# Two cached attention layers, decode step: VectorE's code made shorter, probability sums in 128-column matmuls, the last values loaded in five pieces

## The chip, the cores and the metric

The kernel runs on one core of one Trainium2 chip. A core has five engines with their own instruction streams: TensorE (PE; its weight loads are listed as PEld), VectorE (DVE), ScalarE (ACT), GpSimd (POOL) and SyncE (SP). Sixteen DMA engines carry its transfers. The metric is the device time of one execution in microseconds (us). Before the change the median of four runs is 441.03 us (440.8 to 441.29).

## The reference

Two layers of grouped-query attention for one new token each (batch 4, 32 query heads, 8 key/value heads, 128 wide) over a cache of 8192 positions. Layer A reads the whole cache, layer B only its last W = 2048 positions. Both outputs are put side by side.

```python
q = (x @ wq) split into heads                       # x: [4, 1, 512], wq: [512, 4096]
k, v = cache, repeated for the 4 query heads of each key/value head
scores = einsum("bhqd,bhkd->bhqk", q, k) * 128 ** -0.5
p = softmax(scores)
o = einsum("bhqk,bhkd->bhqd", p, v) @ wo            # wo: [4096, 512]
```

All inputs are bfloat16. Keys and values of layer A are 134 MB, of layer B (the window) 34 MB, the four weight matrices 17 MB: 184.56 MB are read in all.

## The kernel before, in words

The work is cut into 20 units. Units 0 to 3 are layer B, one batch entry each with all eight key/value heads; units 4 to 19 are layer A, one pair of key/value heads of one batch entry each. A unit reads 4 MB of keys (`K_sb`) and 4 MB of values (`V_sb`), each in one of two slots. Its 128 tiles hold 64 positions of two heads.

Per unit, TensorE transposes the keys through PSUM (`pe_T`, line 278), eight tiles a job; VectorE and ScalarE take turns in copying them to `KT_sb` (lines 286 and 287). TensorE forms the scores against the unit's queries (`pe_S`, line 309) in the banks `SA` and `SB`. VectorE takes the maxima (line 411), GpSimd combines them over the partitions (line 432), VectorE subtracts (lines 439 and 449), and ScalarE takes the exponential into `PT` (line 460). One unit later TensorE adds up the probabilities against a matrix of ones (`pe_SM`, line 337; 16 matmuls of `NW = 64` columns, four accumulation groups), VectorE reduces that to a sum per head (`dve_sum`, line 467, `LB` from 256 columns) and inverts it (line 474), TensorE multiplies probabilities and values (`pe_PV`, line 325), and VectorE normalizes (`add_norm`, lines 482 to 497). A turn is two units. Each turn also turns eight heads' outputs (`pe_job_OT`, `pe_job_OL`; copies at lines 354 and 374) and multiplies them with a piece of `wo` (`pe_job_OPJ`, line 387, added up in `oacc` at line 395). In the turns 0 to 2 there is no piece yet, and these jobs work on zeros.

The order of every engine's work is written out by hand in `plan` (one list per engine). `emit_loop` (line 817) emits it: TensorE's ten turns are a hardware loop; VectorE and ScalarE run turns 0 to 2 unrolled and turns 3 to 9 as a loop. GpSimd's and SyncE's code is unrolled throughout. At the end of each turn a loop subtracts the turn's count from every semaphore that it waits on, with one instruction per semaphore (line 883). A wait that is implied by an earlier wait of the same engine on the same semaphore is not emitted.

Ahead of the first unit stands the set-up. GpSimd clears buffers and makes the identity matrices (lines 513 to 531). VectorE writes the masks and the permutation matrix (lines 533 to 554), and copies the Q projection out of PSUM: `xT` (line 203), `QT` (line 226, four jobs per layer) and `RQ` (line 248, four casts per layer). The Q weights lie in the slots of `V_sb` meanwhile, so that the first values can be loaded only when their projection is done (line 721).

SyncE issues all large loads in one queue, in the order K of the unit, then V of the unit before (lines 745 to 763). A K load waits until the slot's keys have been transposed (`T`) or its older unit has been normalized (`otr`), a V load waits for `otr` of two units before. The values of the last unit come in four transfers (`VCH = [4, 2, 1, 1]`, line 682, in eighths of 4 MB), each with a semaphore of its own, then eight transfers of 128 KB with the last piece of `wo` (`Wl_sb`). After the loops TensorE runs PV of the last unit in eight chunks, each waiting for its transfer; ahead of the fifth chunk it adds the probabilities (`pe_SM(L)`) and loads `oacc` into the accumulators (`pe_seed`). Then come the last normalization (line 488), 16 matmuls with `Wl_sb` (line 699), two copies (lines 703 and 704) and two output transfers.

Of the kernel before, what the change touches and what calls it, by code (L numbers as in the profile page):

```python
# [9 lines left out]
ACTF = mybir.ActivationFunctionType  # L10
# [4 lines left out]
def bass_concat_heads__gqa_block_cached__sliding_block_cached__decode_kernel(  # L15
# [33 lines left out]
    scale = float(DH) ** -0.5  # L49
    NKT = 4  # L50
    NW = 64
    NBK = 4
    NFILL = 3
    NTH = NT // 2
# [16 lines left out]
    with ExitStack() as es:  # L71
# [8 lines left out]
        def sm(name):  # L80
# [39 lines left out]
        KTB = [ps("KT%d" % i, 512) for i in range(NBK)]  # L120
        OTB = ps("OT", 512)

        names = ["k0", "k1", "kh", "v0", "v1", "vl0", "vl1", "vl2", "vl3", "wl0", "wl1", "wl2", "wl3", "wl4", "wl5", "wl6", "wl7", "x0", "x1", "w0", "w1", "wo",
                 "out0", "out1", "out2", "Tq", "Td", "Ta", "S", "PV", "Ed", "Ea", "Eq", "max", "sub", "sum", "rcp", "exp", "otr", "os", "otp",
                 "ocp", "Ef", "fin0", "fin1", "ar1", "SM", "maxc", "pset", "setup", "pm0", "pm1", "oc", "ocB", "mk0", "mk", "mka", "perm", "rq"]
        sems = {n: sm("s_" + n) for n in names}

        K_sbf = K_sb.bitcast(F32)
# [6 lines left out]
        def sem_of(key):  # L135
            t = key[0]
            if t in ("K", "Kh"):
                return sems["k%d" % (key[1] % 2)]
            if t in ("V", "Vh"):
                return sems["v%d" % (key[1] % 2)]  # L140
            if t == "T":
                j = jobs[key[1]]
                return sems["Tq" if j["turn"] is None else "Td" if j["eng"] == "dve" else "Ta"]
            if t == "pm":
                return sems["pm%d" % key[2]]
            if t == "KH":
                return sems["kh"]
            if t in ("VL", "WL", "x", "out", "fin"):
                return sems["%s%d" % (t.lower(), key[1])]
            if t == "WQ":  # L150
                return sems["w%d" % key[1]]
            if t == "E":
                if jobs[key[1]]["turn"] is None:
                    return sems["Eq"]
                return sems["Ed"] if jobs[key[1]]["eng"] == "dve" else sems["Ea"]
            return sems[t]

        DMA_KEYS = ("K", "Kh", "KH", "V", "Vh", "VL", "WL", "x", "out", "WQ", "wo", "mk")

# [28 lines left out]
            return KTB[jobs[idx]["bank"]]  # L188

        def pe_job_xT(P):  # L190
            idx = xt_idx[P] = new_job("xT", "dve")
            bk = kbank(idx).bitcast(BF16)

            def fn(pe):
                ins = None
                for c in range(DC):
                    ins = pe.transpose(out=bk[:, c * 8:c * 8 + Bn], in_=x_sb[0:Bn, P, :].rearrange("b (p c) -> b c p", c=DC)[:, c, :],  # L197
                                       identity=ident[0:Bn, 0:Bn])
                return ins
            op("pe", fn, waits=[("x", P), ("setup",), bankfree(idx)], inc=("T", idx))  # L200

            def efn(dve):
                return dve.tensor_copy(out=xT[:, P, :, :],
                                       in_=bk[:, 0:DC * 8].rearrange("p (c b) -> p c b", c=DC)[:, :, 0:Bn])
            add(dict(eng="dve", fn=efn, waits=[("T", idx)], inc=("E", idx)))

        def wq_view(P):
            return V_sb[:, 1 - P, :, :].rearrange("p t d -> p (t d)").rearrange("p (c n) -> p c n", c=DC)

        def pe_job_QP(P, i):  # L210
            idx = qp_idx[(P, i)] = new_job("QP", "dve")
            bk = kbank(idx)
            wv = wq_view(P)

            def fn(pe):
                ins = None
                for hl in range(HQJ):
                    hq = i * HQJ + hl
                    for c in range(DC):
                        ins = pe.matmul(out=bk[:, hl * Bn:(hl + 1) * Bn], lhsT=wv[:, c, hq * DH:(hq + 1) * DH],  # L220
                                        rhs=xT[:, P, c, :], start=(c == 0), stop=(c == DC - 1))
                return ins
            op("pe", fn, waits=[("WQ", P), ("E", xt_idx[P]), bankfree(idx)], inc=("T", idx))

            def efn(dve):
                return dve.tensor_copy(out=QT[:, P, :, i * HQJ:(i + 1) * HQJ],
                                       in_=bk[:, 0:HQJ * Bn].rearrange("p (h b) -> p b h", b=Bn))
            add(dict(eng="dve", fn=efn, waits=[("T", idx)], inc=("E", idx)))

        def pe_job_perm(P):  # L230
            idx = perm_idx[P] = new_job("perm", "dve")
            bk = kbank(idx)

            def fn(pe):
                ins = None
                for e in range(2):
                    ins = pe.matmul(out=bk[:, e * Bn * HQ:(e + 1) * Bn * HQ],
                                    lhsT=permE[:, e, :, :].rearrange("p t i -> p (t i)"),
                                    rhs=QT[:, P, :, :].rearrange("p b h -> p (b h)"), start=True, stop=True)
                return ins  # L240
            op("pe", fn, waits=[("E", qp_idx[(P, NQP - 1)]), ("perm",), bankfree(idx)], inc=("T", idx))

            def efn(dve):
                ins = None
                for e in range(2):
                    for tl in range(2):
                        src = bk[64 * tl:64 * tl + 64, e * Bn * HQ:(e + 1) * Bn * HQ]
                        ins = dve.tensor_copy(
                            out=RQ[P][64 * tl:64 * tl + 64, :, :, e, C * tl:C * tl + C],
                            in_=src.rearrange("p (b g c) -> p b g c", b=Bn, g=NSEG))  # L250
                return ins
            add(dict(eng="dve", fn=efn, waits=[("T", idx)], inc=("E", idx)))

        def pe_filler(n):
            bank = (jobs[-1]["bank"] + 1) % NBK
# [74 lines left out]
        def pe_SM(u):  # L330
            def fn(pe):
                ins = None
                for s in range(NSEG):
                    n = TS * C // NW
                    for i in range(n):
                        c0 = s * TS * C + i * NW
                        ins = pe.matmul(out=SA[u % 2][:, s * NW:(s + 1) * NW], lhsT=onesb[:, :], rhs=PT[:, u % 2, c0:c0 + NW],  # L337
                                        start=(i == 0), stop=(i == n - 1))
                return ins
            op("pe", fn, waits=[("exp", u) if u >= 0 else None], inc=("SM", u))  # L340
# [18 lines left out]
        def pe_job_OL(tn):  # L359
# [9 lines left out]
            op("pe", fn, waits=[("E", ot_idx[tn]), bankfree(idx)], inc=("T", idx))  # L369

            def efn(dve):
                ins = None
                for h in range(REP):
                    ins = dve.tensor_copy(
                        out=OL[32 * h:32 * h + 32, :, :, :],
                        in_=bk[32 * h:32 * h + 32, 0:REP * NR].rearrange("p (r g h b) -> p g h r b", r=REP, g=2, h=REP)[:, :, h, :, :])
                return ins
# [85 lines left out]
        def dve_sum(u):  # L463
            S, n = nseg(u), ncol(u)

            def fn(dve):
                return dve.tensor_reduce(out=LB[:, 0:n].rearrange("p (s h) -> p s h", h=C),
                                         in_=SA[u % 2][:, 0:NSEG * NW].rearrange("p (s j h) -> p s h j", s=S, h=C),
                                         axis=AX.X, op=AluOpType.add)
            return dict(eng="dve", fn=fn, waits=[("SM", u)], inc=("sum", u))  # L470

# [32 lines left out]
        def pool_otp(tn):  # L504
# [5 lines left out]
                w.append(("otr", 2 * tn - 2))  # L510
            return dict(eng="pool", fn=lambda pool: pool.tensor_copy(out=OTp[:, :, :], in_=OT_sb[:, P, q, :, :]), waits=w, inc=("otp", tn))

        def pool_setup0(pool):
            pool.memset(dummy[:, :], 0.0)
            pool.memset(onesf[:, :], 1.0)
# [4 lines left out]
            pool.memset(oacc[:, :], 0.0)  # L520
            pool.memset(PT[:, :, :], 0.0)
            return pool.memset(Wo_sb[:, :, :, :], 0.0)
        op("pool", pool_setup0, inc=("pset",))

        def pool_setup1(pool):
            ins = pool.affine_select(out=ident[:, :], in_=onesb[:, :], pattern=[[1, 128]],
# [3 lines left out]
            return ins  # L530
        op("pool", pool_setup1, waits=[("pset",)], inc=("setup",))

        def dve_setup0(dve):
            mkv = MK[:, :].rearrange("p (g s h) -> p g s h", g=NSEG, s=2)
            dve.memset(mkv[0:64, :, 0, :], 0.0)
            dve.memset(mkv[0:64, :, 1, :], -BIG)
            dve.memset(mkv[64:128, :, 0, :], -BIG)
            return dve.memset(mkv[64:128, :, 1, :], 0.0)
        op("dve", dve_setup0, inc=("mk0",))

        def dve_setup1(dve):
            dve.memset(MASK[0][0:64, 0:REP], 0.0)
            dve.memset(MASK[0][0:64, REP:C], -BIG)
            dve.memset(MASK[0][64:128, 0:REP], -BIG)
            return dve.memset(MASK[0][64:128, REP:C], 0.0)
        op("dve", dve_setup1, inc=("mka",))

        def dve_setup2(dve):
            ins = None
            for e in range(2):  # L550
                for tl in range(2):
                    ins = dve.tensor_copy(out=permE[:, e, tl, :], in_=ident[:, :].rearrange("p (i e) -> p e i", e=2)[:, e, :])
            return ins
        op("dve", dve_setup2, waits=[("setup",)], inc=("perm",))
        for sh in range(2):
            m0 = MASK[1][:, :]
            pstm = m0.ap[0][0]
# [121 lines left out]
            return ins  # L679
        add(dve_sum(L))  # L680
        add(dve_rcp(L))
        VCH = [4, 2, 1, 1]
        vch_of = [i for i, n in enumerate(VCH) for _ in range(n)]
        for c in range(NC):
            w = [("VL", vch_of[c])]
# [246 lines left out]
```

## Time and profile before

| what | value |
|---|---|
| median of four runs | 441.03 us (440.8 to 441.29) |
| profiled execution, its own time | 441.43 us |
| its span, first to last instruction | 439.6 us |
| granted TensorE clock, mean | 0.957 |
| read from HBM | 184.56 MB, 420 GB/s over the span |
| VectorE, line 286, 160 copies | 110.5 us, 690 ns each |
| VectorE, line 467, 20 reductions | 8.4 us, 418 ns each |
| VectorE, line 411 on `SB`, 20 reductions | 13.8 us, 692 ns each |
| VectorE, line 374, 40 casts | 7.4 us, 184 ns each |
| VectorE, line 226, 8 casts | 1.5 us, 192 ns each |
| VectorE, line 248, 8 casts | 2.3 us, 288 ns each |
| TensorE, line 337, 336 matmuls | 13.2 us, 192 ns each (they overlap) |

The span is the stretch between the first and the last instruction of the profiled execution; 1.83 us of its time lie around it. Busy times are summed per group of instructions. Matmuls are pipelined, so their durations overlap. Instructions are fetched by DMA too: the list of DMA queues shows them as kind "instruction". The trace also holds a record of every single DMA packet (start, duration, size and queue), and each transfer ends with a four-byte completion write from each DMA engine that took part in it.

### The profile page before, as it was taken

What the parts mean: (1) busy time and instruction counts of PE and PEld (TensorE: products, weight loads), DVE (VectorE), ACT (ScalarE), POOL (GpSimd) and SP (SyncE); (2) the same over time, 40 slices, a digit from 0 to 9 for tenths busy, and PEclk for the clock granted to TensorE, in tenths of its full rate; (3) what the DMA queues carried; (4) which work ended last, traced back from release to release, by engine and by line L of the source; (5) the groups of instructions that cost most, each with busy time, mean ns of one, the idle gap of its engine ahead of it and who ended that gap; (6) DMA issues with size and microseconds to landing.
All of it is one profiled execution on the core that took longest, in us unless ns stands there. A gap on an engine that the chain in (4) does not pass through costs nothing.

```text
span 439.6 us, 15852 instructions
## 1 busy us (share of the span) xinstructions
PE 365.5 (83%) x7312; PEld 337.2 (77%) x7312; DVE 210.2 (48%) x462; ACT 189.7 (43%) x203; POOL 27.8 (6%) x84
## 2 busy tenths in 40 slices
PE   0068998998997958895989698969878895989986
PEld 0068897997996948795979688968878794979975
DVE  0034455654664634463555346625653563555641
ACT  1004473473563625271636263534534361636530
POOL 6100000000000000000000000000100000000000
PEclk9999999999999988998899799969998998899999
DMA  8999999999999999999999999999999999999995
GB/s 341 421 416 419 418 418 420 422 444 409 448 429 432 416 441 429 432 424 435 429 435 423 430 438 425 433 432 429 414 445 432 435 423 436 429 429 413 446 407 210
DMA packets 13253, 184.76 MB, mean 420 GB/s; under 512 B 1412, under 2 KB 2488, under 8 KB 4536
## 3 DMA queue, kind: packets, MB, share of 16 engines
q1 hardware_dynamic: 13152, 184.56, 99.0%
q8 instruction: 8, 0.13, 0.1%
q14 instruction: 5, 0.04, 0.0%
q0 software_dynamic: 64, 0.02, 0.0%
q10 hardware_dynamic: 24, 0.01, 0.0%
HBM read 184.56 MB, written 0.01 MB: 420 GB/s over the span
## 4 chain that ended last, share of the span: by engine, by line
DMA 46%; PE 45%; PEld 4%; issue 2%; DVE 1%; SPq 1%; PEldq 0%
DMA K_sb<-in_A_k_cache_dram 35%; PE KT L278 23%; PE OT L325 9%; DMA K_sb<-in_B_k_cache_dram 7%; DMA V_sb<-in_A_v_cache_dram 4%; PE SA L309 4%; PE SB L309 4%; PE KT L387 3%; PEld KT L278 2%; SPq L566 1%; PE SA L337 1%; PE KT L325 1%; DVE oacc L395 1%; PEld OT L325 1%; PEld SA L309 1%
## 5 line engine op out<-in xcount | busy, mean ns | idle before, releaser
L278 PE MATMUL KT<-identf,K_sb 128*128 128x128 f32 x1280 | 207.5, 296 | 45.1 <-DMA K_sb<-in_A_k_cache_dram 34.0
L287 ACT ACTIVATE KT_sb<-KT 128x1024 bf16<-128x1024 bf16 x160 | 163.2, 1024 | 137.8 <-PE KT L278 137.8
L278 PEld LDWEIGHTS KT<-identf,K_sb 128*128 128x128 f32 x1280 | 146.9, 149 | 50.6 <-DMA K_sb<-in_A_k_cache_dram 35.3
L286 DVE COPY KT_sb<-KT 128x512 int32<-128x512 int32 x160 | 110.5, 690 | 120.8 <-PE KT L278 119.3
L325 PE MATMUL OT<-PT,V_sb 128*128 128x64 bf16 x2560 | 78.1, 193 | 2.1 <-DMA V_sb<-in_A_v_cache_dram 1.2
L325 PEld LDWEIGHTS OT<-PT,V_sb 128*128 128x128 bf16 x2560 | 75.9, 98 | 2.4 <-DMA V_sb<-in_A_v_cache_dram 1.3
L460 ACT ACTIVATE PT<-Dt 128x512 bf16<-128x512 f32 x40 | 24.6, 631 | 80.5 <-DVE Dt L449 80.5
L309 PEld LDWEIGHTS SA<-RQc,KT_sb 128*128 128x128 bf16 x1280 | 57.0, 98 | 2.4
L309 PEld LDWEIGHTS SB<-RQc,KT_sb 128*128 128x128 bf16 x1280 | 50.6, 97 | 7.9 <-issue 4.4
L309 PE MATMUL SA<-RQc,KT_sb 128*128 128x16 bf16 x1280 | 56.4, 170 | 0.0
L309 PE MATMUL SB<-RQc,KT_sb 128*128 128x16 bf16 x1280 | 52.8, 170 | 0.0
L411 DVE TENSOR_REDUCE M<-SB 128x8 f32<-128x512 f32 (+1 forms) x20 | 13.8, 692 | 50.3 <-PE SB L309 50.3
L432 POOL PARTITION_ALL_REDUCE MB<-M1m x20 | 7.7, 387 | 334.8 <-DVE M1m L425 334.8
L387 PE MATMUL KT<-Wo_sb,OL 128*4 128x512 bf16 x80 | 18.9, 379 | 0.0
L197 PE MATMUL KT<-ident,x_sb 4*128 4x4 bf16 x8 | 0.6, 170 | 20.8 <-POOL identf L528 20.8
L197 PEld LDWEIGHTS KT<-ident,x_sb 4*128 4x128 bf16 x8 | 0.4, 113 | 21.0 <-issue 21.0
L449 DVE TENSOR_TENSOR Dt<-SA,MBm 128x512 f32<-128x512 f32 x20 | 13.8, 691 | 0.7
L449 DVE TENSOR_TENSOR Dt<-SB,MBm 128x512 f32<-128x512 f32 x20 | 13.6, 681 | 0.0
L411 DVE TENSOR_REDUCE M<-SA 128x8 f32<-128x512 f32 (+1 forms) x20 | 13.6, 681 | 0.0
L337 PE MATMUL SA<-PT,onesb 128*128 128x64 bf16 x336 | 13.2, 192 | 0.0
L387 PEld LDWEIGHTS KT<-Wo_sb,OL 128*4 128x4 bf16 x80 | 6.0, 84 | 8.1
L337 PEld LDWEIGHTS SA<-PT,onesb 128*128 128x128 bf16 x336 | 11.1, 97 | 0.0
(72 smaller groups left out, 125.7 us busy)
## 6 DMA issues: line engine op xcount, KB each, us to landing
K_sb<-in_A_k_cache_dram SPq DMA_DIRECT2D x15, 4096.0 KB, 22.7
V_sb<-in_A_v_cache_dram SPq DMA_DIRECT2D x15, 4096.0 KB, 30.8
K_sb<-in_B_k_cache_dram SPq DMA_DIRECT2D x16, 1024.0 KB, 22.8
V_sb<-in_B_v_cache_dram SPq DMA_DIRECT2D x16, 1024.0 KB, 19.4
V_sb<-in_B_wq_dram SPq DMA_DIRECT2D x1, 4096.0 KB, 12.6
V_sb<-in_A_wq_dram SPq DMA_DIRECT2D x1, 4096.0 KB, 22.5
Wo_sb<-in_B_wo_dram SPq DMA_DIRECT2D x4, 1024.0 KB, 11.8
K_sb<-in_A_k_cache_dram SPq DMA_DIRECT2D x2, 2048.0 KB, 18.5
```

Of the source, the lines that this page charges most:

```text
L278: ins = pe.transpose(out=bkf[:, pi * 128:(pi + 1) * 128], in_=K_sbf[:, slot, t0:t0 + 2, :].rearrange("p t d -> p (t d)"), identity=identf[ ...
L286: return e.tensor_copy(out=KT_sb.bitcast(I32)[:, tj % NKT, :], in_=bkf.bitcast(I32)[:, :])
L287: return e.activation(out=KT_sb[:, tj % NKT, :], in_=bk[:, :], func=ACTF.Copy)
L309: ins = pe.matmul(out=stb[:, t % NTH * C:(t % NTH + 2) * C], lhsT=ktv[:, pi, :, e], rhs=RQc[:, u % 2, t // TS, e, :], start=(e == 0), stop ...
L325: ins = pe.matmul(out=otb[:, s * NW:s * NW + w], lhsT=V_sb[:, slot, t, :], rhs=PT[:, slot, t * C:t * C + w], start=(j == 0), stop=(j == n ...
L337: ins = pe.matmul(out=SA[u % 2][:, s * NW:(s + 1) * NW], lhsT=onesb[:, :], rhs=PT[:, u % 2, c0:c0 + NW], start=(i == 0), stop=(i == n - 1))
L387: ins = pe.matmul(out=bk[0:Bn, 0:D], lhsT=OL[:, i // REP, i % REP, :], rhs=Wo_sb[:, i // REP, i % REP, :], start=(i == 0), stop=(i == C - 1))
L395: return dve.tensor_tensor(out=oacc[:, :], in0=bk[0:Bn, 0:D], in1=oacc[:, :], op=AluOpType.add)
L411: return dve.tensor_reduce(out=M1[:, h * n:(h + 1) * n].rearrange("p (s h) -> p s h", h=C), in_=bank[:, :].rearrange("p (s j h) -> p s h j ...
L432: return pool.partition_all_reduce(MB[:, 0:n], M1m[:, 0:n], channels=128, reduce_op=ReduceOp.max)
L449: return dve.tensor_tensor(out=Dt[:, h * NTH * C:(h + 1) * NTH * C].rearrange("p (s j h) -> p s j h", s=Sh, h=C), in0=bank[:, :].rearrange ...
L460: return act.activation(out=PT[:, u % 2, a:b], in_=Dt[:, a:b], func=ACTF.Exp, scale=scale)
```

## The change

The 12 set-up instructions of VectorE (masks and permutation matrix) go to GpSimd; the mask writes stand ahead of its other set-up, the permutation copies behind the identity matrices. The Q projection's copies out of PSUM go to ScalarE, and the four casts to `RQ` become two. In the turns without a piece of `wo`, the four copies to `OL` become one of the same number of elements. The semaphores `max`, `maxc`, `sum`, `rcp` and `os`, with which VectorE waits for itself, become one, `vs`. The probability sums go in 8 matmuls of `NM = 128` columns in place of 16 of 64, and the reduction behind them reads 512 columns in place of 256. The last values come in five transfers, `[2, 2, 2, 1, 1]`.

```diff
+    NM = 128
...
-                 "out0", ..., "Eq", "max", "sub", "sum", "rcp", "exp", "otr", "os", "otp",
+                 "out0", ..., "Eq", "vs", "sub", "exp", "otr", "otp",
...
-            return sems[t]
+            return sems["vs" if t in ("max", "maxc", "sum", "rcp", "os") else t]
...
-            def efn(dve):
-                return dve.tensor_copy(out=QT[:, P, :, i * HQJ:(i + 1) * HQJ],
-                                       in_=bk[:, 0:HQJ * Bn].rearrange("p (h b) -> p b h", b=Bn))
-            add(dict(eng="dve", fn=efn, waits=[("T", idx)], inc=("E", idx)))
+            def efn(act):
+                return act.activation(out=QT[:, P, :, i * HQJ:(i + 1) * HQJ],
+                                      in_=bk[:, 0:HQJ * Bn].rearrange("p (h b) -> p b h", b=Bn), func=ACTF.Copy)
+            add(dict(eng="act", fn=efn, waits=[("T", idx)], inc=("E", idx)))
...
+                for tl in range(2):
+                    ins = act.activation(
+                        out=RQ[P][64 * tl:64 * tl + 64, :, :, :, C * tl:C * tl + C].rearrange("p b g e c -> p e (b g) c"),
+                        in_=bk[64 * tl:64 * tl + 64, 0:2 * Bn * HQ].rearrange("p (e s c) -> p e s c", e=2, c=C), func=ACTF.Copy)
...
-                    n = TS * C // NW
+                    n = TS * C // NM
                     for i in range(n):
-                        c0 = s * TS * C + i * NW
-                        ins = pe.matmul(out=SA[u % 2][:, s * NW:(s + 1) * NW], lhsT=onesb[:, :], rhs=PT[:, u % 2, c0:c0 + NW],
+                        c0 = s * TS * C + i * NM
+                        ins = pe.matmul(out=SA[u % 2][:, s * NM:(s + 1) * NM], lhsT=onesb[:, :], rhs=PT[:, u % 2, c0:c0 + NM],
...
             def efn(dve):
+                if tn not in pieces:
+                    return dve.tensor_copy(out=OL[:, :, :, :].rearrange("p g r b -> p (g r b)"), in_=bk[:, 0:NR])
...
-                                         in_=SA[u % 2][:, 0:NSEG * NW].rearrange("p (s j h) -> p s h j", s=S, h=C),
+                                         in_=SA[u % 2][:, 0:NSEG * NM].rearrange("p (s j h) -> p s h j", s=S, h=C),
...
+        op("pool", pool_mask0, inc=("mk0",))
...
+        op("pool", pool_mask1, inc=("mka",))
...
-        op("pool", pool_setup0, inc=("pset",))
+        op("pool", pool_setup0, waits=[("mk0",), ("mka",)], inc=("pset",))
...
-        op("dve", dve_setup2, waits=[("setup",)], inc=("perm",))
+        op("pool", pool_perm, waits=[("setup",)], inc=("perm",))
...
-        VCH = [4, 2, 1, 1]
+        VCH = [2, 2, 2, 1, 1]
```

More of the change, by code (lines that the diff above doesn't have):

```diff
@@ L121, in bass_concat_heads__gqa_block_cached__sliding_block_cached__decode_kernel @@
         OTB = ps("OT", 512)
-        names = ["k0", "k1", "kh", "v0", "v1", "vl0", "vl1", "vl2", "vl3", "wl0", "wl1", "wl2", "wl3", "wl4", "wl5", "wl6", "wl7", "x0", "x1", "w0", "w1", "wo",
-                 "out0", "out1", "out2", "Tq", "Td", "Ta", "S", "PV", "Ed", "Ea", "Eq", "max", "sub", "sum", "rcp", "exp", "otr", "os", "otp",
-                 "ocp", "Ef", "fin0", "fin1", "ar1", "SM", "maxc", "pset", "setup", "pm0", "pm1", "oc", "ocB", "mk0", "mk", "mka", "perm", "rq"]
+        names = ["k0", "k1", "kh", "v0", "v1", "vl0", "vl1", "vl2", "vl3", "vl4", "wl0", "wl1", "wl2", "wl3", "wl4", "wl5", "wl6", "wl7", "x0", "x1", "w0", "w1", "wo",
+                 "out0", "out1", "out2", "Tq", "Td", "Ta", "S", "PV", "Ed", "Ea", "Eq", "vs", "sub", "exp", "otr", "otp",
+                 "ocp", "Ef", "fin0", "fin1", "ar1", "SM", "pset", "setup", "pm0", "pm1", "oc", "ocB", "mk0", "mk", "mka", "perm", "rq"]
         sems = {n: sm("s_" + n) for n in names}
@@ L190, in pe_job_xT @@
         def pe_job_xT(P):
-            idx = xt_idx[P] = new_job("xT", "dve")
+            idx = xt_idx[P] = new_job("xT", "act")
             bk = kbank(idx).bitcast(BF16)
@@ L200, in pe_job_xT @@
             op("pe", fn, waits=[("x", P), ("setup",), bankfree(idx)], inc=("T", idx))
-            def efn(dve):
-                return dve.tensor_copy(out=xT[:, P, :, :],
-                                       in_=bk[:, 0:DC * 8].rearrange("p (c b) -> p c b", c=DC)[:, :, 0:Bn])
-            add(dict(eng="dve", fn=efn, waits=[("T", idx)], inc=("E", idx)))
+            def efn(act):
+                return act.activation(out=xT[:, P, :, :],
+                                      in_=bk[:, 0:DC * 8].rearrange("p (c b) -> p c b", c=DC)[:, :, 0:Bn], func=ACTF.Copy)
+            add(dict(eng="act", fn=efn, waits=[("T", idx)], inc=("E", idx)))
         def wq_view(P):
@@ L210, in pe_job_QP @@
         def pe_job_QP(P, i):
-            idx = qp_idx[(P, i)] = new_job("QP", "dve")
+            idx = qp_idx[(P, i)] = new_job("QP", "act")
             bk = kbank(idx)
@@ L223, in pe_job_QP, with efn @@
             op("pe", fn, waits=[("WQ", P), ("E", xt_idx[P]), bankfree(idx)], inc=("T", idx))
-            def efn(dve):
-                return dve.tensor_copy(out=QT[:, P, :, i * HQJ:(i + 1) * HQJ],
-                                       in_=bk[:, 0:HQJ * Bn].rearrange("p (h b) -> p b h", b=Bn))
-            add(dict(eng="dve", fn=efn, waits=[("T", idx)], inc=("E", idx)))
+            def efn(act):
+                return act.activation(out=QT[:, P, :, i * HQJ:(i + 1) * HQJ],
+                                      in_=bk[:, 0:HQJ * Bn].rearrange("p (h b) -> p b h", b=Bn), func=ACTF.Copy)
+            add(dict(eng="act", fn=efn, waits=[("T", idx)], inc=("E", idx)))
         def pe_job_perm(P):
-            idx = perm_idx[P] = new_job("perm", "dve")
+            idx = perm_idx[P] = new_job("perm", "act")
             bk = kbank(idx)
@@ L241, in pe_job_perm, with efn @@
             op("pe", fn, waits=[("E", qp_idx[(P, NQP - 1)]), ("perm",), bankfree(idx)], inc=("T", idx))
-            def efn(dve):
+            def efn(act):
                 ins = None
[L245 to L250, printed above, removed]
+                for tl in range(2):
+                    ins = act.activation(
+                        out=RQ[P][64 * tl:64 * tl + 64, :, :, :, C * tl:C * tl + C].rearrange("p b g e c -> p e (b g) c"),
+                        in_=bk[64 * tl:64 * tl + 64, 0:2 * Bn * HQ].rearrange("p (e s c) -> p e s c", e=2, c=C), func=ACTF.Copy)
                 return ins
-            add(dict(eng="dve", fn=efn, waits=[("T", idx)], inc=("E", idx)))
+            add(dict(eng="act", fn=efn, waits=[("T", idx)], inc=("E", idx)))
         def pe_filler(n):
@@ L511, in pool_otp, with pool_mask0, pool_mask1 @@
             return dict(eng="pool", fn=lambda pool: pool.tensor_copy(out=OTp[:, :, :], in_=OT_sb[:, P, q, :, :]), waits=w, inc=("otp", tn))
+        def pool_mask0(pool):
+            mkv = MK[:, :].rearrange("p (g s h) -> p g s h", g=NSEG, s=2)
+            pool.memset(mkv[0:64, :, 0, :], 0.0)
+            pool.memset(mkv[0:64, :, 1, :], -BIG)
+            pool.memset(mkv[64:128, :, 0, :], -BIG)
+            return pool.memset(mkv[64:128, :, 1, :], 0.0)
+        op("pool", pool_mask0, inc=("mk0",))
+        def pool_mask1(pool):
+            pool.memset(MASK[0][0:64, 0:REP], 0.0)
+            pool.memset(MASK[0][0:64, REP:C], -BIG)
+            pool.memset(MASK[0][64:128, 0:REP], -BIG)
+            return pool.memset(MASK[0][64:128, REP:C], 0.0)
+        op("pool", pool_mask1, inc=("mka",))
         def pool_setup0(pool):
@@ L531, in bass_concat_heads__gqa_block_cached__sliding_block_cached__decode_kernel, with pool_perm @@
         op("pool", pool_setup1, waits=[("pset",)], inc=("setup",))
[L533 to L548, printed above, removed]
+        def pool_perm(pool):
             ins = None
@@ L551, in dve_setup2 @@
                 for tl in range(2):
-                    ins = dve.tensor_copy(out=permE[:, e, tl, :], in_=ident[:, :].rearrange("p (i e) -> p e i", e=2)[:, e, :])
+                    ins = pool.tensor_copy(out=permE[:, e, tl, :], in_=ident[:, :].rearrange("p (i e) -> p e i", e=2)[:, e, :])
             return ins
-        op("dve", dve_setup2, waits=[("setup",)], inc=("perm",))
+        op("pool", pool_perm, waits=[("setup",)], inc=("perm",))
         for sh in range(2):
```

## The prediction

> **What bounds the kernel now.** I read the slices of the span first, then the DMA queues, then the end of the chain of work, and last the single packet records of the trace.
>
> From the page: the busy shares, the DMA share and the rate in 40 slices, and the queues.
>
> ```profile
> span 439.6 us, 15852 instructions
> ...
> PE 365.5 (83%) x7312; PEld 337.2 (77%) x7312; DVE 210.2 (48%) x462; ACT 189.7 (43%) x203; POOL 27.8 (6%) x84
> ...
> DMA  8999999999999999999999999999999999999995
> GB/s 341 421 416 419 418 418 420 422 444 409 448 429 432 416 441 429 432 424 435 429 435 423 430 438 425 433 432 429 414 445 432 435 423 436 429 429 413 446 407 210
> ...
> q1 hardware_dynamic: 13152, 184.56, 99.0%
> q8 instruction: 8, 0.13, 0.1%
> ...
> q14 instruction: 5, 0.04, 0.0%
> ```
>
> The DMA engines are busy in every slice but the first and the last, and one queue holds 99% of their time. TensorE at 83% looks close, but it waits for loads. A load is also asked for long before its turn: in the chain of waits,
>
> ```profile
> 352.24 20.86 DMA K_sb<-in_A_k_cache_dram
> ```
>
> a 4 MB load needs 20.9 us to land, of which its own packets take 9.7 us (eight rows of 32 KB per DMA engine at 1.21 us each). The rest, about 10 us, it queues. So any engine may be late by some 9 us before DMA runs dry. Only bytes, packet costs, and what follows the last byte set the end.
>
> The end itself, by stretches (the columns end with granted clock, DMA share and GB/s):
>
> ```profile
> 434.50:435.00 0.50, 0.50 (x18) 0.46 (x16) 0.00 (x0) 0.00 (x0) 0.00 (x0) 1.00 0.63 209
> 435.00:435.20 0.20, 0.18 (x7) 0.06 (x3) 0.00 (x0) 0.00 (x0) 0.00 (x0) 1.00 0.20 67
> 435.20:435.60 0.40, 0.10 (x1) 0.11 (x2) 0.18 (x1) 0.00 (x0) 0.00 (x0) 1.00 0.11 38
> 435.60:436.00 0.40, 0.40 (x5) 0.24 (x4) 0.00 (x0) 0.00 (x0) 0.00 (x0) 1.00 0.07 23
> 436.00:436.40 0.40, 0.40 (x6) 0.30 (x5) 0.00 (x0) 0.00 (x0) 0.00 (x0) 1.00 0.07 23
> 436.40:436.70 0.30, 0.30 (x6) 0.23 (x3) 0.00 (x0) 0.00 (x0) 0.00 (x0) 1.00 0.05 17
> ```
>
> One engine of 16 is a share of 0.06. From 435.6 to 436.6 a single DMA engine is still moving the last rows of Wl_sb; the other 15 are done. Every load waits for all 16, so this one sets the end: its last packet ends at 436.63, the last two matmuls of line 699 wait for it (timeline: 437.10, 0.21 us idle for Wl_sb), then 0.41 us of copy, the output transfer, 439.6.
>
> **Why that engine is last.** Each load ends with one completion write per DMA engine, so the packet records give each engine's lag. Lags are constant from load to load (9.71 us for each of 16) except where an instruction fetch falls. The eight q8 fetches (16 KB) strike eight different engines, at about 1.55 us each. The five q14 fetches (8 KB) come at 53.4, 111.5, 151.0, 188.6 and 251.1; those at 111.5, 188.6 and 251.1 cost three different engines 0.68, 0.65 and 0.71. Those at 53.4 and 151.0 both strike the last engine: +0.99 and +0.98. Its lag behind the median engine is 0.67 at 141.9, 1.65 at 154 and 1.73 at 400; the second latest stands at 0.58. VectorE has 52 instruction records ahead of the fetch at 53.4 and 180 ahead of that at 151.0: 128 instructions of 64 bytes are 8 KB. So I take both for VectorE's code.
>
> **The change, part by part**, on the profiled execution: 441.43 = span 439.6 + 1.83 around it; the median of the four runs, 441.03, is 0.40 below.
>
> *VectorE code.* Ahead of its loop stand 170 records, a loop turn has 59, six follow. Gone ahead of the loop: 12 set-up instructions, 18 evacuations of the Q projection, 9 copies of OL (three unrolled turns, 4 to 1), 1 wait, 4 counter corrections (five semaphores become one): 44. In the loop: 2 waits, 4 corrections. So the loop spans 126 to 179 and the code ends near 186, not 236. Each fetch brings a block that is not run yet: VectorE runs on through 151.2 and 152.0 with no gap. The second fetch, asked for at position 180 at the latest, now comes at the loop's end, and its block begins some 116 instructions behind the code instead of 66. I take it that this block is no longer asked for before the end: the last engine's lag falls from 1.73 to 0.75, it stays last by 0.17, all landings after 151 come **0.98** earlier. If it is still fetched, at 186 or 430, the gain is nothing; both ends are kept.
>
> The Trainium skill (Runtime: NRT & Kernel Launch, Instruction fetch mechanics) speaks against this: an engine streams its code in blocks of 16 KiB, needs not fit, and crossing a boundary is mostly hidden. The trace has 8 KB on q14, and hidden from VectorE it is; but not from the DMA engine. By the page this edit is worth nothing and the time is 441.1; by the row 440.1.
>
> *Last values in five transfers.* Eight 16 KB packets per engine (615 ns, 4.92 us) become sixteen of 8 KB (312 ns, 4.99 us), with one more completion write of 9 ns: **+0.08**. TensorE can't use the earlier first piece: after PV of unit 18 its loop-end corrections hold it until 429.5, and the first piece lands at 429.25.
>
> *Sums in 128 columns.* VectorE's sum reads 512 instead of 256 elements per partition: 0.42 becomes 0.68 (row L411, the same reduction over 512). 20 x 0.26 = 5.3 us busy, at most 0.3 per unit, ahead of MBm, both subtractions and exp; next unit's transposes stand behind them. Cover: the 10 us queue. Without it, up to 5.3 us. TensorE: 16 matmuls (0.49 us issued) become 8: between 0.25 and 0.49, so 0 to 0.25 saved, off the path; I take 0.
>
> *Q projection on ScalarE.* Ten evacuations per the two inputs at 0.17 to 0.19 on VectorE; nearest ScalarE rows 0.20 (128x1) and 0.37 (4x256): 0 to +0.2 each. The four casts of 0.29 (1.20 in all) become two: 0.4 to 1.3. GpSimd takes eight memsets (its smallest row is 0.10: up to +0.8, ahead of the identity matrices) and four copies (0.20 to 0.30 each) ahead of two mask transfers, which are needed at 49.8 and landed by 27. Together -1 to +3 us at 33 us. Behind that wait the first transposes, which wait for K_sb until 34.16 anyway, and V(0)'s issue at 25.0, when DMA had loads queued to 42. I take 0; without that cover, +3.
>
> *One chain semaphore* orders VectorE behind itself as its program order does: 0.
>
> At the end TensorE must keep up if landings come 0.98 earlier. PV of 18 starts at 423.4 (it was idle 1.16 us for it), loop end 428.6, four chunks to 430.6, sums and seed 432.0, two chunks 433.0, the others, as they land, 434.0, Wl_sb from 434.3 at 0.11 a matmul: at 435.9 it stands before the last Wl_sb, which comes at 436.2. So the gain arrives: 439.6 - 0.98 + 0.08 = 438.7, with 1.83 440.5, and on the median's footing **440.1**.
>
> **Rivals.**
> 1. *The fetch stays* (later, or in the tail). For: ScalarE has 48 records ahead of its fetch at 111.5 and some 100 instructions in all, so blocks behind an engine's own code are fetched too, there about 75 behind it; VectorE's would start 116 behind. Against: that distance. 441.03 + 0.08 = 441.1.
> 2. *Slower: a block lands on the last engine.* The moved code shifts ScalarE's and GpSimd's fetches earlier and TensorE's code shrinks by 48 instructions. Should one of these strike the last engine, it costs 0.65 to 1.55 with VectorE's fetch gone or not; against the fetch that stays, 441.7 to 442.6. It decides as soon as that engine's lag exceeds 1.73. Against: each queue struck a fixed or a fresh engine so far.
> 3. *VectorE's longer sum becomes the bound* once a load's queueing falls from 10 us to nothing: up to 446.3. Against: it grows by 0.3 per unit and does not add up while DMA is never empty. Under 1 in 50.
>
> **How the numbers follow.** Fetch gone 0.58 (439.8 if the lag falls to the second engine's, 440.5 if TensorE eats half); stays 0.28; a block on the last engine and the rest 0.14. 0.2% of 441.03 is 0.88 us, about what a measurement of this kernel can tell from no change; it lies in the middle of the first case, so faster 0.38, same 0.49, slower 0.13. The range runs from 439.7 to 441.6.
>
> **What would show it.** Right: four q14 fetches ahead of the last 10 us, none of VectorE's between 130 and 430; the last engine alone for under 0.3 us; line 699 ending near 436.5; span near 438.7. Wrong: five q14 fetches, or one DMA engine still alone for a microsecond; any K_sb or V_sb landing that no longer queues; DMA below 9 tenths in a middle slice.

## The result, and the profile after

The changed kernel takes **440.21 us** (median of 38 runs, 439.95 to 440.98); the kernel before, run beside it, 441.16 (58 runs, 440.64 to 442.56). The ratio is 0.9979, 95% interval [0.9974, 0.9984]: 0.95 us less, where the prediction had 0.90 less. The profiled execution took 440.20, of which 438.4 are its span.

From the page of the changed kernel: instructions, the busy shares, DMA by slices, and the queues.

```profile
span 438.4 us, 15458 instructions
...
PE 366.0 (84%) x7144; PEld 337.6 (77%) x7144; DVE 207.8 (47%) x423; ACT 192.9 (44%) x217; POOL 29.0 (7%) x96
...
DMA  8999999999999999999999999999999999999996
GB/s 336 431 417 419 418 419 421 420 440 413 446 431 431 417 444 431 431 431 431 431 431 431 431 431 431 431 431 431 408 453 431 431 428 431 434 431 413 446 404 253
...
q1 hardware_dynamic: 13296, 184.56, 99.2%
q8 instruction: 8, 0.13, 0.1%
q14 instruction: 4, 0.03, 0.0%
```

The bound is the same: DMA is busy in every slice, with the same bytes on q1. In the DMA row only the last slice is fuller (6 tenths for 5, and 253 GB/s for 210): the transfers are done sooner, and the span ends sooner behind them. Of the five q14 fetches four are left, and the one that is missing is VectorE's second. The packet records have the four at 85.3, 90.9, 110.1 and 247.5 us, VectorE's at 90.9.

Loads still queue for some 10 us. From the chain of waits (start, length, what):

```profile
351.82 20.01 DMA K_sb<-in_A_k_cache_dram
```

The end, by stretches (PE, PEld, DVE, ACT, POOL busy; granted clock, DMA share, GB/s):

```profile
434.80:435.20 0.40, 0.40 (x6) 0.19 (x3) 0.00 (x0) 0.00 (x0) 0.00 (x0) 1.00 0.32 108
435.20:435.60 0.40, 0.40 (x5) 0.12 (x4) 0.00 (x0) 0.00 (x0) 0.00 (x0) 1.00 0.04 13
435.60:436.00 0.40, 0.40 (x5) 0.14 (x4) 0.00 (x0) 0.00 (x0) 0.00 (x0) 1.00 0.00 0
```

Before, one DMA engine (a share of 0.06) worked alone for a microsecond, to 436.6. Now a single engine works for less than the stretch from 435.2 to 435.6, and after 435.6 nothing is moved. TensorE still ends with waits for the last weights, so it is still the transfers that set the end. From the timeline (start, busy, engine, line, and in brackets the idle time and what ended it):

```profile
435.26 0.08 PEld L700 LDWEIGHTS KT<-Wl_sb,OT_sb 128*4 128x4 bf16 x1 [0.21 <-DMA Wl_sb<-in_A_wo_dram]
...
435.57 0.08 PEld L700 LDWEIGHTS KT<-Wl_sb,OT_sb 128*4 128x4 bf16 x1 [0.22 <-DMA Wl_sb<-in_A_wo_dram]
...
435.88 0.08 PEld L700 LDWEIGHTS KT<-Wl_sb,OT_sb 128*4 128x4 bf16 x1 [0.22 <-DMA Wl_sb<-in_A_wo_dram]
...
436.74 0.28 SPq L567 DMA_DIRECT2D out_dram<-osb  x1
```

The changed groups, from the page and from the full list of groups (busy, mean ns of one):

```profile
L468 DVE TENSOR_REDUCE LB<-SA 128x8 f32<-128x512 f32 (+1 forms) x20 | 13.7, 684 | 2.8 <-PE SA L336 2.8
...
L336 PE MATMUL SA<-PT,onesb 128*128 128x128 bf16 x168 | 12.7, 218 | 0.0
```

```profile
L227 ACT ACTIVATE QT<-KT 128x32 bf16<-128x32 f32 x8 | 1.6, 197 | 6.4 <-PE KT L221 6.4
L247 ACT ACTIVATE RQ<-KT 64x256 bf16<-64x256 f32 x4 | 1.5, 378 | 1.0 <-PE KT L238 1.0
```

VectorE's sum takes 0.684 us for 0.418, half of the matmuls are gone, and ScalarE's copies cost 197 and 378 ns each.

### The profile page after: what moved, and what is told of

Read it like the earlier page. It is cut to its first block, busy times and chain, and to the rows that moved or that the text cites. A ratio compares the mean times of both kernels' runs of the same rounds, so it can differ in the third digit from the quotient of the medians.

```text
span 438.4 us, 15458 instructions
## 1 busy us (share of the span) xinstructions
PE 366.0 (84%) x7144; PEld 337.6 (77%) x7144; DVE 207.8 (47%) x423; ACT 192.9 (44%) x217; POOL 29.0 (7%) x96
## 4 chain that ended last, share of the span: by engine, by line
DMA 48%; PE 46%; issue 2%; SPq 2%; DVE 1%; PEld 1%; PEldq 0%
DMA K_sb<-in_A_k_cache_dram 34%; PE KT L277 23%; PE OT L324 9%; DMA K_sb<-in_B_k_cache_dram 7%; DMA V_sb<-in_A_v_cache_dram 7%; PE SB L308 4%; PE SA L308 4%; PE KT L388 3%; SPq L567 1%; PE SA L336 1%; DVE oacc L396 1%; PE KT L324 1%; PEld OT L324 1%; DVE OS L493 0%; PE KT L260 0%
## 5 line engine op out<-in xcount | busy, mean ns | idle before, releaser
L468 DVE TENSOR_REDUCE LB<-SA 128x8 f32<-128x512 f32 (+1 forms) x20 | 13.7, 684 | 2.8 <-PE SA L336 2.8
L336 PE MATMUL SA<-PT,onesb 128*128 128x128 bf16 x168 | 12.7, 218 | 0.0
```

The costliest lines, as they stand in the source:

```text
L336: ins = pe.matmul(out=SA[u % 2][:, s * NM:(s + 1) * NM], lhsT=onesb[:, :], rhs=PT[:, u % 2, c0:c0 + NM], start=(i == 0), stop=(i == n - 1))
```

## The experiments

Twelve kernels were run, each beside the kernel before (441.18 to 441.21 us there). The theory was the prediction's: VectorE's second 8 KB block of code, on the DMA engine that is last anyway, sets the end. The rival: some other part of the change gained.

### Code added at the start

Changed kernel, with 50 writes that compute nothing at the head of VectorE's code:

```diff
+        def dve_pad(dve):
+            for i in range(50):
+                ins = dve.memset(Dt[:, i:i + 1], 0.0)
+            return ins
+        op("dve", dve_pad)
```

> The changed kernel, with 50 more VectorE instructions (writes of single columns of a buffer that is unused then) at the very start, where VectorE idles until 35 us. They compute nothing. Theory (the fetch of VectorE's second block of code was what made one DMA engine last): five q14 fetches again, one engine hit twice by 0.98 us, time 0.9 to 1.0 us above the changed kernel: 441.1 to 441.2, ratio to before 0.999 to 1.001. Rivals (the gain comes from the five transfers or from the 128-column sums): the time stays at 440.2, ratio 0.998.

Measured: 440.41 us (440.18 to 440.83), ratio 0.9982 [0.9973, 0.9991], where 441.1 was expected. The second fetch was back (146.5 us), and it cost its DMA engine 0.97 us. But the writes had also moved VectorE's *first* fetch from 90.9 to 6.5 us; what it cost there can't be told from the lags that every execution has by 22 us (this engine's was 0.86). Later than 22 us that engine had one hit and not two, and it ended 0.90 us behind the median engine, against 0.63 for the last engine of the changed kernel. So the run does not test what it was made for.

### Each part alone

The code shortened, with 64-column sums and four last transfers:

```diff
-    NM = 128
+    NM = 64
...
-        VCH = [2, 2, 2, 1, 1]
+        VCH = [4, 2, 1, 1]
```

> The changed kernel with the sums in 64 columns and the last values in four transfers as before: only VectorE's code is shortened. Theory: four q14 fetches, 440.1 to 440.2, ratio 0.9976 to 0.998. Rivals: 441.1, ratio 1.000.

Kernel before, with the last values in five transfers:

```diff
-        VCH = [4, 2, 1, 1]
+        VCH = [2, 2, 2, 1, 1]
```

> The kernel before with the last values in five transfers and nothing else. Theory: 0.08 us more of packet cost, five q14 fetches, ratio 1.000 to 1.0004. Rival (the five transfers are the gain): 440.2, ratio 0.998.

Kernel before, with the 128-column sums (every `NW` in `pe_SM` and `dve_sum` becomes `NM`):

```diff
+    NM = 128
...
-                    n = TS * C // NW
+                    n = TS * C // NM
```

> The kernel before with the sums in 128 columns and nothing else. Theory: hidden, ratio 0.9995 to 1.0005; TensorE's code is 48 instructions shorter, so a fetch of its own may move, with no effect unless it strikes the last engine. Rival (the sums are the gain): 0.998. Rival (VectorE's longer reduction is on the path): above 1.001.

| kernel | us | ratio to before | median span |
|---|---|---|---|
| code shortened alone | 440.74 | 0.9989 [0.9980, 0.9998] | 438.4 |
| five transfers alone | 441.13 | 1.0000 [0.9991, 1.0009] | 439.3 |
| 128-column sums alone | 440.84 | 0.9992 [0.9983, 1.0001] | 439.0 |
| whole change | 440.21 | 0.9979 [0.9974, 0.9984] | 438.4 |
| before, run beside these | 441.18 | 1 | 439.3 |

The transfers alone gain nothing, as expected. The other two miss. The sums alone look 0.34 us better, but their interval reaches 1. The code alone is 0.53 short of the whole change, though its median span is the same, 438.4: it spends 2.42 us outside its span (median of 11 runs), the others 1.73 to 1.85. Its packet records show a q14 fetch of 8 KB at 441.0, 2.2 us behind the end of its span; no other profile has a fetch there. Single executions of other kernels also spend 2.3 us and more outside their spans (two of the changed kernel: 2.28 and 2.45), but their packets are not on record.

Its profile shows a second thing. In the last 16 matmuls (timeline of the weight loads, code shortened alone):

```profile
434.25 0.08 PEld L700 LDWEIGHTS KT<-Wl_sb,OT_sb 128*4 128x4 bf16 x1
435.10 0.08 PEld L700 LDWEIGHTS SA<-Wl_sb,OT_sb 128*4 128x4 bf16 x1 [0.77 <-issue]
```

TensorE stands for 0.77 us with no semaphore to blame. Its last 16 KB block of code comes only after its loop is left; the packet that carries it starts at 432.4 and takes 1.12 us. The five transfers alone have the same gap at the same matmul (0.40 us). The changed kernel has 48 TensorE instructions less ahead of that place (three copies of `pe_SM`, eight matmuls and eight weight loads each), and no gap. So a new rival stood up: the sums gained by moving this edge out of the last matmuls.

### The edge of TensorE's code

Changed kernel, with 24 small matmuls more behind the set-up, 48 instructions (in the second run 56 matmuls, 112 instructions); their results are overwritten:

```diff
+        def pe_pad(pe):
+            for _ in range(24):
+                ins = pe.matmul(out=KTB[3][:, 0:4], lhsT=onesb[:, :], rhs=ident[:, 0:4], start=True, stop=True)
+            return ins
+        op("pe", pe_pad, waits=[("setup",)])
```

> The changed kernel with 24 small TensorE matmuls more, right after the setup (128x4, their results are overwritten): 48 instructions, as many as the 128-column sums take out of TensorE's code. They put the edge of TensorE's last 16 KB block of code back where the kernel before has it, ahead of the fourth matmul of the final group. Theory now held: the sums gained because that edge left the final matmuls; with code shortened and the edge there, TensorE waited 0.77 us at it. Expected 440.6 to 440.9 us and a gap of 0.3 to 0.9 us ahead of the fourth final matmul. Rival (the sums gained by less matmul work or by the other reduction): 440.2 and no gap there.

> The same with 56 small matmuls: the edge moves 64 instructions further up, into the last group of value products, some 29 matmuls before its end. If the block comes when it came before (TensorE resumed at 435.1 us), 29 x 0.033 + 0.3 + 16 x 0.11 us of work stand behind it instead of 12 steps of 0.11: the final matmuls end some 1.2 to 2.0 us later than in the changed kernel. Expected 441.3 to 442.2 us. If instead the block is asked for so much earlier that it comes in time, or the edge isn't what counts: 440.2.

With 24: 440.21 us (440.00 to 440.80), ratio 0.9976 [0.9967, 0.9985]. The gap is there in the profile (timeline of the weight loads):

```profile
434.59 0.08 PEld L705 LDWEIGHTS SA<-Wl_sb,OT_sb 128*4 128x4 bf16 x1
435.21 0.08 PEld L705 LDWEIGHTS KT<-Wl_sb,OT_sb 128*4 128x4 bf16 x1 [0.54 <-issue]
```

and that execution has a span of 438.9; but it is the longest of eleven, whose median is 438.3. So the edge can hold TensorE up, in single executions, and it does not move the median of the changed kernel. The rival falls as the cause of the whole gain.

With 56: 440.24 us (440.02 to 440.70), ratio 0.9980 [0.9971, 0.9990], not 441.3 or more. From its page and from its timeline:

```profile
q8 instruction: 9, 0.15, 0.1%
```

```profile
434.98 0.08 PEld L705 LDWEIGHTS KT<-Wl_sb,OT_sb 128*4 128x4 bf16 x1
435.04 0.09 PEld L705 LDWEIGHTS SA<-Wl_sb,OT_sb 128*4 128x4 bf16 x1
435.32 0.08 PEld L705 LDWEIGHTS KT<-Wl_sb,OT_sb 128*4 128x4 bf16 x1 [0.19 <-DMA Wl_sb<-in_A_wo_dram]
```

My placing of the edge was wrong. With that much more code TensorE fetches one block more, early (at 75 us), and nothing is missing at the end. A ninth TensorE block, on an engine that is not last, costs nothing that shows here.

### VectorE's second fetch put back where it was

Changed kernel, with 50 VectorE writes in turn 2, so that the first fetch stays in its place:

```diff
+            if u == 5:
+                def dve_pad(dve):
+                    for i in range(50):
+                        p = 32 * (i % 4)
+                        ins = dve.memset(LB[p:p + 32, C + i // 4:C + i // 4 + 1], 0.0)
+                    return ins
+                op("dve", dve_pad, waits=[("rcp", 3)])
```

> The changed kernel with 50 VectorE writes more (into columns of LB that this phase doesn't use; they compute nothing), placed in turn 2, so that the first block of VectorE's code is fetched where it was (about 91 us) and the second fetch comes back at 130 to 155 us, on the same DMA engine. Theory: that engine then has its start lag and two hits of 0.98 us, 2.3 to 2.7 us in all, against some 2.0 of an engine that a TensorE block hit: 440.5 to 440.9. If a VectorE fetch costs its full 0.98 us: 441.2. If the gain of the shortening has another cause than the fetch: 440.2.

Measured: **440.89 us** (440.67 to 441.38), ratio 0.9994 [0.9985, 1.0003]; the interval lies just above that of the changed kernel (to 0.9984). The fifth q14 fetch is back, and so is the engine that works alone. The writes themselves are busy for 3.0 us, 59 ns each, and follow each other every 95 ns, 4.7 us from first to last; DMA's row stays at 9 tenths in every middle slice, so this is hidden. From the group list, the page and the stretches:

```profile
L637 DVE MEMSET LB<- 32x1 f32 x50 | 3.0, 59 | 1.8
```

```profile
DMA  8999999999999999999999999999999999999996
...
q14 instruction: 5, 0.04, 0.0%
```

```profile
435.60:436.00 0.40, 0.40 (x6) 0.27 (x4) 0.00 (x0) 0.00 (x0) 0.00 (x0) 1.00 0.07 23
436.00:436.40 0.40, 0.40 (x5) 0.09 (x2) 0.00 (x0) 0.00 (x0) 0.00 (x0) 1.00 0.01 3
```

So one block of VectorE's code, with nothing else of the change undone, gives back 0.68 of the 0.95 us (0.8 of 0.95 in the median span).

Changed kernel with four transfers:

```diff
-        VCH = [2, 2, 2, 1, 1]
+        VCH = [4, 2, 1, 1]
```

> The changed kernel with the last values in four transfers (4, 2, 1, 1 pieces) as before. TensorE then starts on unit 18's tail later, but waits for the last output weights anyway: 440.1 to 440.3 (no more than 0.1 either way) by the theory that the DMA engines set the end; if the five transfers carried part of the gain, 440.5 to 440.8.

Measured: 440.23 us (439.86 to 440.55), ratio 0.9978 [0.9969, 0.9987]. The five transfers carry nothing.

### A third block, the sums once more, both undone, another engine's block

Changed kernel with 178 writes, 89 ahead of unit 5 and 89 ahead of unit 6:

```diff
+            if 5 <= u < 7:
...
+                    for i in range(89):
+                        p = 32 * (i % 4)
+                        buf = LB[p:p + 32, :] if u == 5 else RL[p:p + 32, 0, :]
+                        ins = dve.memset(buf[:, C + i // 4:C + i // 4 + 1], 0.0)
```

> The changed kernel with 178 VectorE writes more (into unused columns of LB and RL; they compute nothing), half ahead of unit 5 and half ahead of unit 6: one 8 KB block of code more than with 50. Theory: a third fetch of VectorE on the same DMA engine, which is already the last there, so the full 0.98 us more than with 50 writes (440.89): 441.8 to 441.95 us, and span 440.0 to 440.2. If the time follows the writes' own duration or the length of the code: some other step; if the fetches are not what counts: 440.9 or less.

Measured: 447.49 us (446.11 to 448.22), far above 441.9. The writes were meant to be a cheap carrier of code. They were not (timeline of VectorE, and the group list):

```profile
150.72 8.41 DVE L636 MEMSET RL<- 32x1 f32 x89
...
L636 DVE MEMSET RL<- 32x1 f32 x89 | 5.3, 59 | 3.2
```

Each half lasts 8.4 us (the first from 123.9 to 132.3): a write is busy for 59 ns, but the next one starts 95 ns after it. The K and V slots came free so late that DMA ran dry (stretches):

```profile
174.00:176.00 2.00, 2.00 (x76) 2.00 (x72) 1.86 (x7) 0.00 (x0) 0.37 (x1) 1.00 0.04 16
176.00:178.00 2.00, 2.00 (x53) 2.00 (x50) 1.43 (x5) 1.23 (x2) 0.21 (x2) 1.00 0.00 0
```

The third fetch came (163.9 us, +1.01 on the same engine), but the run says nothing of its price. It says what the prediction's cover is worth: two lumps of 8.4 us, 18 us apart, are more than a queue of 10 us hid.

Changed kernel with 64-column sums again, and 32 small matmuls that move TensorE's edge:

```diff
-    NM = 128
+    NM = 64
...
+            for _ in range(32):
+                ins = pe.matmul(out=KTB[3][:, 0:4], lhsT=onesb[:, :], rhs=ident[:, 0:4], start=True, stop=True)
```

> The changed kernel with the probability sums back in 64-column matmuls, and 32 small TensorE matmuls more after the setup, which put TensorE's code edge where it makes no wait. In the earlier run of the code shortened alone, the median span was that of the changed kernel (438.4), and 0.6 us came after the span, with a code fetch at 441.4. Theory: the sums are worth nothing once that fetch is gone: span 438.3 to 438.5 and 440.15 to 440.3 us. Rival (64-column sums cost 0.5 us by themselves): 440.7.

Measured: 440.27 us (440.00 to 440.84), ratio 0.9980 [0.9971, 0.9988], median span 438.4 with 1.84 us outside it. The 0.5 us that the shortened code alone had lost are gone, with the sums still in 64 columns. With TensorE's edge out of the way the sums are worth nothing.

Changed kernel with the 50 writes and the 24 matmuls, that is, both edges of code back:

```diff
+            if u == 5:
...
+                op("dve", dve_pad, waits=[("rcp", 3)])
...
+        op("pe", pe_pad, waits=[("setup",)])
```

> The changed kernel with both undone as code only: 50 VectorE writes in turn 2 and 24 TensorE matmuls after the setup. Theory: TensorE's wait at the code edge is hidden behind the late DMA engine, so the time is that with the 50 writes alone, 440.85 to 441.0; if the two add up, 441.1 to 441.3, which would be all of the kernel before.

Measured: 441.10 us (440.54 to 441.52), ratio 0.9998 [0.9989, 1.0006], median span 439.35, the same as before. That is 0.21 above the writes alone, as if the two added up, and a gap of 0.24 us stands in its final matmuls; but the two intervals overlap.

Changed kernel with 12 GpSimd writes more in each of ten units, into a tile that is no longer read:

```diff
+            if 5 <= u < 15:
...
+                    for i in range(12):
+                        ins = pool.memset(RQ[1][:, 0, (u - 5) % 4, (u - 5) // 4 % 2, i:i + 1] if u < 13 else RQ[1][:, 1, u - 13, 0, i:i + 1], 0.0)
```

> The changed kernel with 120 GpSimd writes more, 12 in each of ten units, into a tile no longer read (they compute nothing): GpSimd's code grows by about one 8 KB block, fetched in the loaded stretch. Theory: a fetch costs only where it falls on the engine that is last; GpSimd's cost 0.7 us on an engine of their own: 440.2 to 440.35 us. If any fetch delays the loads by its length: 440.9.

Measured: 440.43 us (440.12 to 440.69), ratio 0.9982 [0.9973, 0.9991], a little over the expectation. The fetch came at 289.2 us and cost its engine 0.66. In the profiled execution this made that engine, until then level with the median, the last by 0.2 (0.63, the next 0.41); the median time is 0.22 above the changed kernel's. So a block costs what it adds to the *latest* engine: here 0.2, not 0.66 and not 0.

### All profiles side by side

The packet records give the lags of the 16 DMA engines; a load is there when the last engine has finished. The records name no engine: one is followed by its lag from packet to packet. Of each profiled execution but that with 178 writes (lags in us behind the median engine at the values of unit 17; then when the last engine finished the values of unit 18):

| kernel | VectorE fetches later than 22 us | last engine | next | values of 18 done | span | span less that |
|---|---|---|---|---|---|---|
| before | 2 | 1.73 | 0.57 | 423.9 | 439.6 | 15.7 |
| five transfers alone | 2 | 1.42 | 0.54 | 423.4 | 439.3 | 15.9 |
| sums alone | 2 | 1.24 | 0.50 | 423.5 | 439.1 | 15.6 |
| 50 writes and 24 matmuls | 2 | 1.33 | 0.30 | 423.4 | 439.2 | 15.8 |
| 50 writes in turn 2 | 2 | 1.17 | 0.49 | 423.3 | 439.0 | 15.7 |
| 50 writes at the start | 1 | 0.90 | 0.41 | 422.9 | 438.7 | 15.7 |
| changed | 1 | 0.63 | 0.36 | 422.6 | 438.4 | 15.7 |
| GpSimd's block | 1 | 0.63 | 0.41 | 422.7 | 438.5 | 15.7 |
| 56 matmuls | 1 | 0.58 | 0.31 | 422.7 | 438.5 | 15.8 |
| sums back, edge moved | 1 | 0.41 | 0.22 | 422.4 | 438.2 | 15.8 |
| four transfers | 1 | 0.36 | 0.34 | 422.4 | 438.0 | 15.7 |
| code alone (gap 0.77) | 1 | 0.58 | 0.33 | 422.7 | 438.8 | 16.1 |
| 24 matmuls (gap 0.54) | 1 | 0.79 | 0.25 | 422.9 | 438.9 | 16.0 |

The last column hardly moves: 15.6 to 15.9 us lie between the last engine's landing and the end, whatever the kernel, and 0.3 more in the two executions in which TensorE waited long at its code edge. Every kernel with two fetches of VectorE later than 22 us has a last engine at 1.17 or more; with one fetch none is above 0.90.

## Why the prediction was right, and where it was not

**The bound: right.** The slowest of 16 DMA engines sets the end (table above).

**The lost fetch: right as the mechanism, too large as a term.** The fetch went, and putting it back undoes 0.68 us of the change. The prediction took 0.98, all that the packet row shows, with the sentence that the last engine "stays last by 0.17". It does not: in the changed kernel VectorE's engine ends 0.3 behind the median, and another is last at 0.63, one that a TensorE block struck (1.56) on top of a lag of 0.44 from the start. In the profile of before, 1.18 us of VectorE's engine's lateness were there at 22 us, ahead of both hits, and were chance: in the four other profiles of the table with two fetches it stands at 0.2 to 0.7 there. That lags are the same from execution to execution was assumed from one profile, and is wrong. "Lags are constant from load to load" except at a fetch holds only later than 36 us: between 31.8 and 35.8 us up to six packets of 8 KB in a profile, with no fetch beside them, take 0.47 to 0.96 us where 0.31 is usual (one in the profile of before, three in that of the changed kernel), and these delays stay as well; what causes them is open. So that the sum, 0.90 us, came so near the measured 0.95 is in part luck: its one large term was 0.98, and the runs show 0.68 for it.

The Trainium skill (Runtime: NRT & Kernel Launch, Instruction fetch mechanics) calls the crossing of a block of code mostly hidden. VectorE indeed ran on; the time did not stay the same: 440.21 to 440.89 for one block more. Where page and runs differ, the runs decide.

**The rest of the gain, 0.95 less 0.68 = 0.27 us, points to TensorE's code edge, and is not settled.** The four experiments with two fetches of VectorE fall into two pairs. With the edge among the final matmuls they are near the kernel before (five transfers alone 441.13, 0.05 below it; both edges back 441.10, 0.11 below); without it they are 0.3 below (sums alone 440.84, by 0.34; 50 writes 440.89, by 0.30). But each run by itself is within its interval, and with one fetch the edge costs the median nothing (440.21). Why it should count only when VectorE's engine is late, no run shows. The prediction had this term at nothing.

**Five transfers, +0.08:** not to be seen (441.13 against 441.18; 440.21 against 440.23). **Sums, 0:** right for the time (440.27 with 64 columns), with the reduction at 0.684 us as estimated. The prediction did count the 48 TensorE instructions that go, but only as a fetch that might move; that an edge of code stands inside the last matmuls it did not see. **Q projection, 0:** ScalarE's copies cost 183, 197 and 378 ns, within the bounds, and the first transposes still wait for their keys (to 33.97 us). **The tail:** predicted PV of 18 at 423.4, first `Wl_sb` matmul at 434.3, the last piece at 436.2; it was 423.1, 434.1 and 435.9, and TensorE waits for the last three pieces, where the prediction had it wait for the last.

**What was to be seen:** four q14 fetches, yes; none of VectorE's between 130 and 430, yes; one engine alone for under 0.3 us, yes; the final matmuls ending near 436.5 and a span near 438.7: 436.3 and 438.4, each 0.2 to 0.3 early; the profiled execution of before, from which they were reckoned, had a later engine (1.73) than any other profile of the table (1.42 at most).

**The rivals.** That the fetch stays: no. A block on the last engine: not in this change; GpSimd's block shows its kind at 0.2 us. The longer sum as the bound: no; with 178 writes it took two lumps of 8.4 us of VectorE's time before DMA ran dry.

## What to carry to other kernels

Where DMA is full from end to end, look at the single DMA engines: a transfer is as late as its latest engine, here every block of an engine's code took one of them out for 0.7 to 1.6 us, and that was never made good while the queue was not empty. A block is worth what it adds to the latest engine, which is less than its own length as soon as another is near; so subtract down to the second latest, and take that from several executions and not from one. A change that only makes code shorter or longer can move the time, and so can padding in an experiment: say where each block's fetch falls before you read its time.

## What the hardware showed that was not expected

- VectorE's blocks cost their DMA engine 0.96 to 1.01 us each, while blocks of 8 KB of other engines cost 0.65 to 0.72. They strike the same DMA engine wherever the packets let it be followed (before, the sums alone, both edges back, and the 178 writes with three blocks); with the five transfers alone and with the 50 writes in turn 2 other engines stand within 0.1 us of it, and the records can't tell.
- How late that DMA engine is at 22 us (0.2 to 1.2 us behind the median engine) differs from profile to profile: 1.18 us before and 0.7 or less with the five transfers alone and with the sums alone, although these three kernels run the same code up to then.
- Lags end when the queue runs dry: with the 178 writes, DMA's share fell to 0.62 from 150 to 152 us, and at 155 us all 16 engines stood within 0.4 us of each other, after a spread of 3.1 at 151.
- TensorE's last block comes only after its loop has been left (from 432.2 us on in all profiles of some 440 us); where TensorE met the edge, it went on 1.4 to 1.6 us after the block's packet had ended, and it had stood there for 0.24 to 0.77 us in four profiles.
- A kernel can lose 0.6 us outside its span: the shortened code alone had 2.42 us there (median of 11), for 1.8 of the others, and in its profile a fetch of 8 KB behind the end of its span. Which engine asked for it the trace does not tell.
